# Second block's keys and queries read in fp32 by the SP queue and cast on chip, and the last piece stored from the scalar queue: sliding-window ALiBi attention followed by a squared-ReLU MLP

## The chip, the cores and the metric

The kernel runs on one core of one Trainium2 chip. The metric is the device time of one execution in microseconds (us), the median over several runs. One further execution is recorded by the hardware profiler; its page and its trace are what the text reads. PE is TensorE (matrix multiplies; PEld its weight loads), DVE is VectorE, ACT is ScalarE, POOL is GpSimd, SP is SyncE. A q behind a name is the queue of instructions that starts DMA transfers.

## The reference

Attention with 8 batches, 8 heads, 576 positions and a head size of 64, in a window of 128 positions with an ALiBi bias; its output, as 4608 tokens of 512 values, goes through an MLP with 2048 hidden values:

```python
scores = scale * np.matmul(q, k.transpose(0, 1, 3, 2))
rel = pos[:, None] - pos[None, :]
bias = slopes[:, None, None] * (-np.abs(rel).astype(np.float32))[None, :, :]
mask = (rel >= 0) & (rel < window)
scores = np.where(mask, scores + bias[None], -1000000000.0)
attn = softmax(scores)
x = np.matmul(attn, v)      # heads side by side: (4608, 512)
h = x @ w_in                # (4608, 2048)
r = np.maximum(h, 0.0)
out = ((r * r) @ w_out).astype(np.float32)
```

All inputs and the output are fp32 in memory.

## The kernel before, in words

**Blocks.** Each batch's 576 positions are cut into four blocks of 128 and one of 64. The list `seq` (L197 to L207) has the first blocks of all 8 batches first (numbers m = 0 to 7), then, for two batches at a time, their three middle blocks each ("full" jobs, which see the block before them too) and at last both 64-row ends together (one "half" job). `ranges` gives the order of the 36 tiles of 128 rows in which the MLP takes them; a tile of two halves is two places of 64 rows in the output.

**Attention of a block.** Its k and q go into a bf16 tile `kq`, its v into `vf` or `vt`. For m from 1 on, POOL issues these loads (L387, L392), and its DMA casts fp32 to bf16 on the way. Block 0 differs (`split`, L358 to L382): its k and q are read as fp32 into the tile `stage`, in two halves each, one issued by SP and one by ACT (L373), and DVE casts them into `kq` (L379). k and q are then transposed: for m below `N_PE` by PE with an identity (L443) and copies out of PSUM (L271 on DVE, L273 on ACT), for later blocks by a DMA transpose that SP issues (L429). The scores (L499) go through an exponential on ACT (L523) and a product with a mask on DVE (L531). P times v (L566) has a column of ones that gives the sum, by which DVE divides (L584, L588). The result `x` is transposed into `xT`, by PE (L608) and a copy for m below `N_PE`, in two cuts for m below `N_CUT`, and by a DMA transpose (L596) for the others.

**MLP.** It runs over 9 groups of 512 tokens. The up projection (`h`: L700 in group 0 by units of 128 tokens and 512 hidden values, in groups 1 and 2 by units of 256 tokens; L716 for the later groups) is followed by a ReLU on ACT (L671) and a square on DVE (L662) into `g`. The down projection (`o`, L742) of a tile has four parts of four matmuls, one for each quarter of w_out. A finished tile is copied to `osb` by DVE or ACT (L271, L273) and stored by SP (L761). The last tile is cut at column 384 (`CUT`) into two pieces, each with its own copy and stores. The weights come in four pieces each, cast by POOL's DMA (L340, L343).

**Order.** [...] A planner in the kernel file (class `Plan`) goes through all tasks with estimated durations and writes out one order for each engine. A task has the engines it may run on, a key (a due time, lower first), the tasks it needs and the buffers it takes and frees. On each engine the one with the lowest key is taken among those that could start within `NEAR` ns of the earliest; `LEAD` and `DUE` make the keys of attention blocks, `FIRST` (L16) is the order of the first loads on POOL. Up to eight casting DMAs are in flight in the plan (`LANES`). Where the plan has a hole on PE in its first 30 us, matmuls on a zero tile `warm` (L252) fill part of it. Each engine runs its instructions strictly in that order, with waits on semaphores.

Of the kernel before, what the change touches and what calls it, by code (L numbers as in the profile page):

```python
# [8 lines left out]
FP32 = mybir.dt.float32  # L9
# [5 lines left out]

FIRST = ["b0", "b1", "b2", "i0", "i1", "o0", "i2", "o1", "b3", "i3", "o2", "o3", "b4", "b5", "b6", "b7"]  # L16
DIAG = [[0], [1], [2], [3], [4, 5], [6, 7]]
N_PE = 9
N_CUT = 4
N_PVH = 1  # L20
N_WARM = 8
FILL = 0.7
LEAD = 320
IOTA = 3
# [3 lines left out]
SIZE = {"kq": 4, "v": 9, "kqT": 7, "P": 3, "x": 3}  # L28
DUE = {**{m: 200.0 * m - 1e5 for m in range(40)}, **{7: -40.0}}

# [26 lines left out]
class Plan:  # L57
# [7 lines left out]
    LANES = 8  # L65
    NEAR = {"PE": 25, "ACT": 250, "DVE": 60}
    FILL_UNTIL = 30000.0
# [15 lines left out]

    def order(self):
        used = {tag: [] for tag in self.bufs}
        free, cand, left = {}, {}, {}
# [89 lines left out]
def kernel(  # L176
    ctx: ExitStack, tc: tile.TileContext, q, k, v, moe_w_in, moe_w_out, out
):
    nc = tc.nc
# [20 lines left out]
    for b in range(0, B, 2):  # L200
        for x in [(b + i, kb) for i in range(2) for kb in range(1, HALF)]:
            jobs.append(("full", [len(seq)]))
            seq.append(x)
            ranges.append([x])
        jobs.append(("half", [len(seq), len(seq) + 1]))
        ranges.append([(b, HALF), (b + 1, HALF)])
        seq += ranges[-1]  # L207
    at = {x: m for m, x in enumerate(seq)}
# [27 lines left out]
    xt = ring("x", size["x"], [128, d_model])  # L236
    stage = const.tile([128, 2 * d_model], FP32)

# [18 lines left out]
    def act(n):  # L257
        return n * 0.95 + 115.0
# [43 lines left out]

    t_dist, t_mask, last_mask = [None, None], [[], []], None
    for part in (1, 0):
        key = EARLY + 2 if part else -1e5 + 1100
        t_dist[part] = plan.add({"DVE": 430.0}, key, lambda part=part: build_dist(part), [t_ident], name="dist",
                                later=0.0 if part else 18000.0)
        for p in range(H):
            def build_mask(p=p, part=part):
                nc.scalar.activation(masks[:, p, part], dist[:, part], AF.Exp, bias=0.0,  # L310
                                     scale=-(2.0 ** (-8.0 * (head_at[p] + 1) / H)))
            t_mask[part].append(plan.add({"ACT": act(128)}, key + 1 + p, build_mask, [t_dist[part]], name="mask"))

    def ones(ts):
        for t in ts:
            nc.vector.memset(t[:, :, D:D + 1], 1.0)
    t_ones = [plan.add({"DVE": 320.0}, EARLY + 3, lambda: ones(tiles["v0"][0:2]), name="ones"),
              plan.add({"DVE": 900.0}, -1e5 + 300, lambda: ones(tiles["v0"][2:]), name="ones", later=11000.0),
              plan.add({"DVE": 1200.0}, -1e5 + 900, lambda: ones(tiles["v"]), name="ones", later=20000.0)]

# [36 lines left out]
    def load_block(m, key):  # L357
        kb = seq[m][1]  # L358
        n = blk[kb]
        ns = 870.0 * n / 128  # L360
        split = m == 0
        s_kq[m], s_v[m] = Slot("kq"), Slot("v" if kb else "v0")
# [4 lines left out]

        if m == 0:
            t_l = []
            for i, src in enumerate((k, q)):  # L370
                for r, (eng, e) in enumerate((("SP", nc.sync), ("ACTQ", nc.scalar))):
                    def fetch(i=i, src=src, r=r, e=e):
                        e.dma_start(view(stage, i)[:, r], source(src, m, split)[:, :, r])  # L373
                    t_l.append(plan.add({eng: 450.0}, key + 0.1 * i, fetch, dma=330.0, lat=1000.0,
                                        name=f"l{'kq'[i]}{m}.{r}"))

            def cast_kq(i):
                w = slice(i * d_model, (i + 1) * d_model)
                nc.vector.tensor_copy(kq[s_kq[m].idx][:, w].rearrange("s (i r d) -> s r i d", i=4, d=D),  # L379
                                      stage[:, w].rearrange("s (r i d) -> s r i d", r=2, d=D))  # L380
            c_k = plan.add({"DVE": 480.0}, key, lambda: cast_kq(0), t_l[0:2], [s_kq[m]], name=f"ck{m}")
            c_q = plan.add({"DVE": 480.0}, key, lambda: cast_kq(1), t_l[2:4] + [c_k], name=f"cq{m}")  # L382
            t_kq[m] = [c_k, c_q]
# [38 lines left out]
    def transpose_kq(m, due):  # L422
        n = blk[seq[m][1]]
        kb = seq[m][1]
        sT = s_kqT[m] = Slot("kqT" if kb else "kqT0")
        split = m == 0
        if m >= N_PE:
# [7 lines left out]
        for i in range(2):  # L435
# [14 lines left out]
            for c0, c1 in pieces:  # L450
                def evac(i=i, st=st, c0=c0, c1=c1, e=len(evs[i])):
# [4 lines left out]
                    else:  # L456
# [3 lines left out]
                evs[i].append(plan.add({"ACT": act(w), "DVE": dve_p(w, 1 if split else 2)}, due - 58, evac,  # L460
                                       [t_tp[i]] + evs[i], [], [st], name=f"ev{m}.{i}"))
        last["tp"] = t_tp[1]
# [175 lines left out]
    def blocks(lo, hi):  # L638
        return [at[x] for r in range(lo // 128, hi // 128) for x in ranges[r]]
# [10 lines left out]

    g_slots, g_sq, o_slots = {}, {}, {}

    def relu_square(g, slot, last_mm, key, out_of, fused):
# [12 lines left out]
        else:  # L666
            srt = Slot("rt")

            def relu():
                srt.tile = work.tile([128, 512], BF16, tag="rt", bufs=3, name="rt")  # L670
                nc.scalar.activation(srt.tile, slot.tile, AF.Relu, bias=0.0, scale=1.0)  # L671
            tr = plan.add({"ACT": act(512)}, key, relu, [last_mm], [srt], [slot], name=f"relu{g}")
            ts = plan.add({"DVE": dve(512, 2)}, key, lambda: square(srt.tile), [tr] + g_sq[g][:1], [], [srt],
                          name=f"sq{g}")
        g_sq[g].append(ts)
# [10 lines left out]
    def unit(g, r, e, key):  # L686
# [8 lines left out]
        def emit():  # L695
            fill(t_mm, bank_of(slot, "h"))
            for f in range(nf):
                fc = nf * e + f
                for cc in range(C):
                    nc.tensor.matmul(slot.tile[:, f * w:(f + 1) * w], w_in_sb[:, cc, fc * 128:(fc + 1) * 128],  # L700
                                     xT[:, cc, lo:lo + w], start=cc == 0, stop=cc == C - 1)
        t_mm = plan.add({"PE": 4 * nf * mm(w)}, key, emit,
                        [t_win[nf * e // 4]] + [x for m in ms for x in t_x[m]], [slot] + new, name=f"u{g}.{r}.{e}")
        ts = relu_square(g, slot, t_mm, key,
# [4 lines left out]
    def fc_step(g, fc, key):  # L709
# [3 lines left out]
        def emit():  # L713
            bank(slot, "h")
            for cc in range(C):
                nc.tensor.matmul(slot.tile, w_in_sb[:, cc, fc * 128:(fc + 1) * 128],  # L716
                                 xT[:, cc, g * 512:(g + 1) * 512], start=cc == 0, stop=cc == C - 1)
        t = plan.add({"PE": 4 * mm(512)}, key, emit,
                     [t_win[fc // 4]] + [x for m in blocks(g * 512, g * 512 + 512) for x in t_x[m]], [slot] + new,
                     name=f"fc{g}.{fc}")  # L720
        ts = relu_square(g, slot, t, key, lambda gt: gt[:, fc, :], FUSED(g, fc))
# [10 lines left out]
    def o_piece(g, t, some, key, z, lo, hi, end):  # L732
# [4 lines left out]
        def emit():  # L737
# [3 lines left out]
            for fc in range(4 * some[0], 4 * some[-1] + 4):  # L741
# [3 lines left out]
                      [prev] + [x for p in some for x in [t_wout[p]] + sq_of[g, t, p]],  # L745
                      [slot] if some[0] == 0 else [], [g_slots[g]] if t == 3 and some[-1] == 3 and end else [],
                      name=f"o{g}.{t}.{some[-1]}")
        o_slots[g, t, z][1] = tm
# [4 lines left out]
        def evac():  # L753
            so.tile = work.tile([128, d_model], FP32, tag="osb", bufs=3, name="osb")
            copy(te, so.tile[:, 0:hi - lo], slot.tile[:, 0:hi - lo])
        te = plan.add({"ACT": act(hi - lo), "DVE": dve_p(hi - lo)}, key, evac, [tm], [so], [slot], name=f"oe{g}.{t}")

        def store():
            for i, (b, kb) in enumerate(ranges[4 * g + t]):
                n = blk[kb]  # L760
                nc.sync.dma_start(out[b * S + kb * 128:b * S + kb * 128 + n, lo:hi],  # L761
                                  so.tile[i * 64:i * 64 + n, 0:hi - lo])
        plan.add({"SP": 530.0}, key, store, [te], [], [so], dma=680.0 * (hi - lo) / 512, lat=1000.0, name=f"st{g}.{t}")

# [38 lines left out]
```

The softmax here doesn't subtract the row's maximum and nothing guards it: scores larger than these inputs give would overflow.

## Time and profile before

| | |
|---|---|
| median of 5 runs | 317.56 us (317.14 to 317.71) |
| the profiled execution's own time | 317.25 us |
| its span, first to last instruction | 315.5 us |
| PE, DVE, ACT, POOL busy | 306.4, 173.1, 173.5, 105.5 us |
| DMA packets | 164130, of which 154752 under 512 B |
| first matmul of the up projection | 14.07 us |
| last matmul | ends at 310.8 us |

The page has the busy time of each engine, the span in 40 slices, the DMA queues, the chain of work that ended last, and groups of instructions by line. Other views of the same trace are a timeline, the waits of an engine (who waited for whom, total us, times, longest us) and busy times in stretches of one's choice. A matmul's end is modelled by the profiler, so that PE can be busy without running at its peak; the step from one matmul's start to the next one's tells its true cost. In lists of DMA, MB count the bytes written.

### The profile page before, as it was taken

To read this page: it belongs to the slowest core of one execution; us is meant where nothing else is said; L and a number is where in the kernel's file an instruction comes from. 1 tells how busy PE (TensorE), PEld (TensorE's weight loads), DVE (VectorE), ACT (ScalarE), POOL (GpSimd) and SP (SyncE) were. 2 spreads that over 40 slices of the span, in tenths; PEclk is the share of its full clock that TensorE was granted. 3 is DMA by queue.
4 is the path that set the end of the run, shared out by engine and by line. 5 is a ranking of instruction groups with operands and counts; after the bars stand their busy time and mean duration, and the time that the engine had idled before them with its cause. 6 is when DMAs were issued, how large, how long until landed. Compare 5 with 4: busy or idle time off the path is not lost.

```text
span 315.5 us, 7140 instructions
## 1 busy us (share of the span) xinstructions
PE 306.4 (97%) x2810; PEld 176.4 (56%) x2810; DVE 173.1 (55%) x494; ACT 173.5 (55%) x340; POOL 105.5 (33%) x131
## 2 busy tenths in 40 slices
PE   6999999999999999999999999999999999999994
PEld 3877768667777655555554455545444444444442
DVE  3755577566767667676666666666663222222111
ACT  4675466668566636675656665547743444444300
POOL 8825498643623845206746007200000000000000
PEclk9999999999999999999999999999999999999998
DMA  9999999999999999959999949962211000011112
GB/s 130 189 202 190 170 195 175 145 168 144 221 160 129 179 165 177 156 96 140 167 195 164 138 98 132 193 115 70 50 52 50 35 34 33 35 33 45 56 69 67
DMA packets 164130, 39.14 MB, mean 124 GB/s; under 512 B 154752, under 2 KB 159616, under 8 KB 164096
## 3 DMA queue, kind: packets, MB, share of 16 engines
q0 software_dynamic: 114656, 18.10, 84.3%
q1 hardware_dynamic: 49152, 20.33, 33.4%
q8 instruction: 22, 0.36, 0.5%
q10 hardware_dynamic: 288, 0.26, 0.3%
q14 instruction: 12, 0.10, 0.1%
HBM read 36.70 MB, written 9.44 MB: 146 GB/s over the span
## 4 chain that ended last, share of the span: by engine, by line
PE 88%; DMA 8%; POOL 2%; issue 0%; DVE 0%; POOLq 0%
PE o L742 39%; PE h L716 27%; PE h L700 11%; PE pv L566 6%; PE s L499 5%; DMA w_out_sb<-in_moe_w_out_dram 5%; DMA w_in_sb<-in_moe_w_in_dram 3%; POOL kq L387 1%; POOL vf L392 1%; PE tp L443 1%; PE xp L608 0%; POOL w_in_sb L340 0%; POOL dist L287 0%; DVE osb L271 0%; POOLq L287 0%
## 5 line engine op out<-in xcount | busy, mean ns | idle before, releaser
L742 PE MATMUL o<-w_out_sb,g 128*128 128x512 bf16 (+2 forms) x592 | 143.0, 373 | 0.3 <-DMA w_out_sb<-in_moe_w_out_dram 0.3
L671 ACT ACTIVATE rt<-h 128x512 bf16<-128x512 f32 x144 | 85.8, 609 | 94.5 <-PE h L716 69.9
L662 DVE TENSOR_TENSOR g<-rt 128x512 bf16<-128x512 bf16 x144 | 60.2, 421 | 75.9 <-ACT rt L671 75.8
L716 PE MATMUL h<-xT,w_in_sb 128*128 128x512 bf16 x384 | 96.7, 379 | 0.0
L742 PEld LDWEIGHTS <-g 128*128 128x128 bf16 x592 | 54.1, 98 | 56.0 <-issue 0.4
L523 ACT ACTIVATE P<-s 128x512 bf16<-128x512 f32 (+1 forms) x136 | 67.0, 582 | 9.2 <-PE s L499 9.2
L716 PEld LDWEIGHTS <-w_in_sb 128*128 128x128 bf16 x384 | 35.2, 98 | 39.3
L531 DVE TENSOR_TENSOR P<-P,masks 128x512 bf16<-128x512 bf16 (+1 forms) x112 | 44.6, 405 | 15.7 <-ACT P L523 11.0
L700 PE MATMUL h<-xT,w_in_sb 128*128 128x128 bf16 (+1 forms) x512 | 46.7, 246 | 1.2 <-DMA w_in_sb<-in_moe_w_in_dram 0.7
L392 POOL DMA_DIRECT2D vt<-in_v_dram x32 | 27.1, 849 | 49.5 <-PE pv L566 46.5
L387 POOL DMA_DIRECT2D kq<-in_k_dram x39 | 33.4, 857 | 30.4 <-DMA kqT<-kq 23.8
L700 PEld LDWEIGHTS <-w_in_sb 128*128 128x128 bf16 x512 | 38.6, 98 | 5.2 <-DMA w_in_sb<-in_moe_w_in_dram 1.6
L387 POOL DMA_DIRECT2D kq<-in_q_dram x39 | 33.6, 861 | 8.8 <-DMA w_out_sb<-in_moe_w_out_dram 5.2
L588 DVE TENSOR_TENSOR x<-pv,rec 128x256 bf16<-128x256 f32 (+1 forms) x80 | 33.6, 422 | 2.6
L566 PEld LDWEIGHTS <-P 128*128 128x128 bf16 (+1 forms) x576 | 25.7, 101 | 15.3 <-DVE x L588 1.7
L584 DVE RECIPROCAL rec<-pv 128x4 f32<-128x4 f32 (+1 forms) x80 | 14.3, 179 | 20.9 <-PE pv L566 18.0
L566 PE MATMUL pv<-vt,P 128*128 128x65 bf16 (+1 forms) x448 | 24.6, 194 | 0.0
L273 ACT ACTIVATE osb<-o 128x512 f32<-128x512 f32 x23 | 13.9, 606 | 8.0 <-PE o L742 7.7
L499 PEld LDWEIGHTS <-kqT 64*128 64x128 bf16 x448 | 12.4, 94 | 7.3 <-issue 7.2
L271 DVE COPY osb<-o 128x512 f32<-128x512 f32 (+2 forms) x14 | 9.2, 654 | 12.8 <-PE o L742 12.6
L499 PE MATMUL s<-kqT 64*128 64x128 bf16 (+1 forms) x256 | 15.6, 210 | 0.0
L499 PE MATMUL s<-kqT,kqT 64*128 64x128 bf16 (+1 forms) x192 | 11.4, 209 | 0.0
(42 smaller groups left out, 102.6 us busy)
## 6 DMA issues: line engine op xcount, KB each, us to landing
out_dram<-osb SPq DMA_DIRECT2D x32, 256.0 KB, 4.0
kq<-in_k_dram POOLq DMA_DIRECT2D x31, 128.0 KB, 7.0
kq<-in_q_dram POOLq DMA_DIRECT2D x31, 128.0 KB, 7.2
vt<-in_v_dram POOLq DMA_DIRECT2D x24, 128.0 KB, 7.2
w_in_sb<-in_moe_w_in_dram POOLq DMA_DIRECT2D x4, 512.0 KB, 10.1
w_out_sb<-in_moe_w_out_dram POOLq DMA_DIRECT2D x4, 512.0 KB, 15.1
vf<-in_v_dram POOLq DMA_DIRECT2D x8, 128.0 KB, 6.2
out_dram<-osb SPq DMA_DIRECT2D x6, 128.0 KB, 2.3
```

The lines of the kernel that those rows point to most:

```text
L387: nc.gpsimd.dma_start(view(kq[s_kq[m].idx], i), source(src, m, split))
L392: nc.gpsimd.dma_start(tile_of(s_v[m])[0:n, :, 0:D], source(v, m))
L499: nc.tensor.matmul(sS[2 * g2 + r].tile[:, jj * 256 + c0:jj * 256 + c0 + w], tile_of(s_kqT[mk])[rows, c, :], tile_of(s_kqT[mq])[rows, C + c ...
L523: nc.scalar.activation(flat(Pt[sP.idx]), sS[i].tile.rearrange("p (j t) -> p j t", j=2)[:, :, lo:hi], AF.Exp, bias=0.0, scale=scale)
L531: nc.vector.tensor_tensor(flat(Pt[sP.idx]), flat(Pt[sP.idx]), flat(masks), op=ALU.mult)
L566: nc.tensor.matmul(sv.tile[0:n, hi * (D + 1):(hi + 1) * (D + 1)], Pt[sP.idx][:, place(h)].rearrange("p t q -> p (t q)")[:, w], tile_of(s_v ...
L588: nc.vector.tensor_tensor(xt[sx.idx][0:n, hf * 256:(hf + 1) * 256].rearrange("p (h e) -> p h e", h=4), heads(sv)[0:n, :, 0:D], sr.tile[0:n ...
L662: nc.vector.tensor_tensor(o, i, i, op=ALU.mult)
L671: nc.scalar.activation(srt.tile, slot.tile, AF.Relu, bias=0.0, scale=1.0)
L700: nc.tensor.matmul(slot.tile[:, f * w:(f + 1) * w], w_in_sb[:, cc, fc * 128:(fc + 1) * 128], xT[:, cc, lo:lo + w], start=cc == 0, stop=cc ...
L716: nc.tensor.matmul(slot.tile, w_in_sb[:, cc, fc * 128:(fc + 1) * 128], xT[:, cc, g * 512:(g + 1) * 512], start=cc == 0, stop=cc == C - 1)
L742: nc.tensor.matmul(slot.tile[:, 0:hi - lo], gt[:, fc, t * 128:(t + 1) * 128], w_out_sb[:, fc, lo:hi], start=fc == 0, stop=fc == FCB - 1)
```

## The change

- `split` holds for blocks 0 and 1 (`N_HW` = 2). Block 1's k and q are read as fp32 in two halves each, all four issued by SP, into a second `stage` tile. DVE or ACT casts them. POOL issues only the v of block 1.
- The first loads come in another order: the second piece of w_out and block 3 go ahead of the third piece of w_in.
- `N_PE` goes from 9 to 8, `N_CUT` from 4 to 2, `N_PVH` from 1 to 2 (P times v of block 1 takes a PSUM bank of tag h), `LEAD` from 320 to 440, and `NEAR` is 60 for PE and 0 for ACT. Block 7 loses its own due time.
- A table `ADJ` shifts the keys of some tasks by name. Tasks get distinct names for that.
- For the last two batches the tile of two halves goes one place ahead, so the last tile of all is a full block of 128 rows.
- The last piece of the last tile (columns 384 to 511) is copied by ACT alone and stored from ACT's queue.
- In the plan, a group's first up projection is ordered ahead of its other ones, and `g` is freed only when all four tiles of its group are done.

```diff
-FIRST = ["b0", "b1", "b2", "i0", "i1", "o0", "i2", "o1", "b3", "i3", "o2", "o3", "b4", "b5", "b6", "b7"]
+FIRST = ["b0", "b1", "b2", "i0", "i1", "o0", "o1", "b3", "i2", "i3", "o2", "o3", "b4", "b5", "b6", "b7"]
-N_PE = 9
-N_CUT = 4
-N_PVH = 1
+N_HW = 2
+N_PE = 8
+N_CUT = 2
+N_PVH = 2
-LEAD = 320
+LEAD = 440
-DUE = {**{m: 200.0 * m - 1e5 for m in range(40)}, **{7: -40.0}}
+DUE = {m: 200.0 * m - 1e5 for m in range(40)}
+ADJ = {
+    "ck1": 8900391.0, "e0.3": 100080.3, "e3.2": -142.3, "e3.3": -200, "e6.2": -40, "m1.0": 401.3, "m1.3": 99828.3,
+    "m2.2": 99627.1, "o1.2.0": -479.21, "o2.3.3": -535.5, "pv2.0": -398.2, "r7.0": 789.7, "squ0.0.2": -99571.3,
+    "squ0.1.2": -99827.9, "squ0.2.2": -99869.7, "xp5.0": 98961.41,
+}
-    NEAR = {"PE": 25, "ACT": 250, "DVE": 60}
+    NEAR = {"PE": 60, "ACT": 0, "DVE": 60}
     def order(self):
+        for t in self.tasks:
+            t.key += ADJ.get(t.name, 0.0)
...
-        ranges.append([(b, HALF), (b + 1, HALF)])
-        seq += ranges[-1]
+        seq += [(b, HALF), (b + 1, HALF)]
+        ranges.insert(len(ranges) - (b + 2 == B), seq[-2:])
...
-        split = m == 0
+        split = m < N_HW
...
-                for r, (eng, e) in enumerate((("SP", nc.sync), ("ACTQ", nc.scalar))):
+                for r, (eng, e) in enumerate((("SP", nc.sync), ("SP", nc.sync) if m else ("ACTQ", nc.scalar))):
...
-                nc.vector.tensor_copy(kq[s_kq[m].idx][:, w].rearrange("s (i r d) -> s r i d", i=4, d=D),
-                                      stage[:, w].rearrange("s (r i d) -> s r i d", r=2, d=D))
+                copy((c_k, c_q)[i],
+                     kq[s_kq[m].idx][:, w].rearrange("s (i r d) -> s r i d", i=4, d=D),
+                     stage[:, w].rearrange("s (r i d) -> s r i d", r=2, d=D))
+            engs = {"DVE": 480.0, "ACT": 600.0} if m else {"DVE": 480.0}
...
+        if end and (g, t) == (NG - 1, 3):
+            del engs["DVE"]
...
+        final = end and (g, t) == (NG - 1, 3)
...
-                nc.sync.dma_start(out[b * S + kb * 128:b * S + kb * 128 + n, lo:hi],
-                                  so.tile[i * 64:i * 64 + n, 0:hi - lo])
+                (nc.scalar if final else nc.sync).dma_start(
+                    out[b * S + kb * 128:b * S + kb * 128 + n, lo:hi], so.tile[i * 64:i * 64 + n, 0:hi - lo])
```

## The prediction, made before the changed kernel was run

> **What bounds the kernel now.** I read the page's engine rows first, then what the PE (TensorE) waited for, then the PE by stages of the early part, then the tail.
>
> ```profile
> span 315.5 us, 7140 instructions
> PE 306.4 (97%) x2810; PEld 176.4 (56%) x2810; DVE 173.1 (55%) x494; ACT 173.5 (55%) x340; POOL 105.5 (33%) x131
> ```
>
> PE is the bound; DVE and ACT have 45% spare. But a busy PE need not be doing useful work, so count the work: in the chain of waits four 512-column matmuls take 0.86 us (0.216 each) when nothing stands in their way, and sixteen 128-column ones 0.89 (0.056 each). At these prices PE is without work for 11.5 us up to 14.0, for 3.0 us from 14 to 36, and then for some 0.2 us in each 8 us, up to its last matmul at 310.8. So three stretches can give time back: before the first weights, the 3 us behind them, and the tail.
>
> The waits of PE in the second stretch, and PE in three of its 2 us stages (columns: stage, length, busy, clock, DMA share, GB/s):
>
> ```profile
> PE h L700 <- DMA w_in_sb<-in_moe_w_in_dram: 0.7, 1, 0.7
> PE h L700 <- ACT rt L671: 0.6, 1, 0.6
> PE o L742 <- DMA w_out_sb<-in_moe_w_out_dram: 0.3, 1, 0.3
> ...
> 20.00:22.00 2.00, 1.42 (x10) 1.00 1.24 205
> ...
> 28.00:30.00 2.00, 1.35 (x27) 1.00 1.24 206
> ...
> 32.00:34.00 2.00, 1.69 (x23) 1.00 1.40 205
> ```
>
> Each hole ends when a piece of weights has landed (w_in pieces land at 14.0, 16.6, 21.9, 30.0; w_out at 19.4, 25.1, 32.5, 35.9). The DMA engines never rest meanwhile: the early stage is set by delivery, in the order in which POOL issues. From 36 us PE alone is the bound.
>
> The tail, by the timeline:
>
> ```profile
> 310.56 1.13 SPq L761 DMA_DIRECT2D out_dram<-osb  x2
> 310.87 0.29 DVE L271 COPY osb<-o 128x128 f32<-128x128 f32 x1 [0.33 <-PE o L742]
> ...
> 311.79 1.19 SPq L761 DMA_DIRECT2D out_dram<-osb  x2
> ```
>
> The last copy ends at 311.16, but its two stores stand behind the two of the larger piece on SP; the last is issued at 312.39, lands at 314.30, and 1.16 us of closing steps make 315.46. Outside the span lie 1.75 us (317.25 profiled); the median is 0.31 above the profiled time, and I carry that along.
>
> **The tail edit.** The last tile becomes a full block, so each of its two pieces is one store of 128 rows in place of two of 64; and the last piece is copied and stored by ACT. The ACT copy of 128 columns is not in the trace: 0.383 us for 256 and 0.606 for 512 give 0.27 by a straight line, against 0.29 on DVE. ACT's queue then has nothing ahead of the store: issue at about 311.2. A 128-row store on SP lands 1.97 us after issue (issued 308.15, landed 310.13), so this one at 313.15 instead of 314.30: **-1.15 us**. The trace has no store from ACT; its nearest row is ACT's first load, landed 2.5 us after issue against 2.2 for the slowest store of this tail, which makes the smaller end -0.85. The larger is -1.4: four of the closing semaphore waits, 0.06 us each, come after the last landing now, and could be done before it. Nothing stands behind it on ACT.
>
> **Block 8 from PE to DMA transposes** (`N_PE` 9 to 8). Removes 8 transposes L443 and 4 of L608, 12 x 0.056 = **-0.67 us**, in a stage where PE is saturated, so all of it counts. It adds two DMA transposes on SP (1.2 to 2.7 us of SP each here), where SP has a store at 47.88 and the next transpose at 51.40. The price is delay: transposes issued at 51.4 to 64.1 land 8.6 to 9.3 us later. Block 8's q lands at 48.75; issued then, its kqT would be there at 57.4 to 58.0, while its scores now run at 55.51. Block 9, already on that route, lands at 60.03 for scores at 62.31, 2.3 us spare, so the written-out order does leave room for it. I take no stall; bounds 0 and +3.9 us (scores placed only the planner's own 5.05 us, 1150 + 1700 + 2200 ns in its constants, behind 48.75).
>
> **Block 1 by SP.** POOL loses two issues (0.89 + 0.90 us), so what stands behind moves up 1.8 us: v of block 1, k, q, v of block 2, and w_in piece 0 (issued 7.66, then about 5.9). SP gains four issues of 0.68 to 0.81 us, about 2.3 to 5.3, behind its two of block 0; its next work was at 39.17, so it is free. What counts is transfer time:
>
> ```profile
> DMA packets 341, 0.32 MB, mean 264 GB/s; under 512 B 32, under 2 KB 341, under 8 KB 341
> q10 hardware_dynamic: 197, 0.19, 56.7%
> ...
> DMA packets 5490, 0.69 MB, mean 154 GB/s; under 512 B 5490, under 2 KB 5490, under 8 KB 5490
> ```
>
> The first two lines are 2.2 to 3.4 us, block 0's fp32 reads; the last is 5.5 to 10, POOL's casting reads. MB are bytes written. Block 1's k and q cost 256 KB in 128 B packets at 154, 1.7 us (the landings step by 0.83 to 0.84 each). In fp32 they are 512 KB in 1 KB packets: 2.0 us at the mean of 264, 1.4 at the 375 of that window's full slices. Here a rule speaks against the edit. The Trainium skill, *DMA: Bandwidth & Descriptors*, "Issuing engines are not separate DMA queues", says that all issuers share the same 16 engines, and a second issuer saves issue time alone. By it nothing but 1.7 becoming 2.0 counts, +0.3 us, since the engines are full from 5 us on. The rows add that they are not full at 2 to 4 (the page's DMA share there is 7 tenths), where SP's new issues begin; and that the packets are eight times larger. I take 1.5 us for the two transfers, w_in piece 0 landing at 13.8 instead of 14.02: **-0.2** (bounds -0.6, +0.5).
>
> The two casts (0.67 and 0.43 us for block 0) go to DVE or ACT; DVE is idle from 6.93 to 8.73 and ACT from 5.1 to 7.04. Without that cover 1.1 us fall on block 1's chain. SP's second load went through, beside POOL's, at 81 packets in half a us (4.5 to 5.0), 0.8 us for its 128 packets; four more from 5.8 end at 9.0 to 9.6, with the cast at about 10.0, where block 1's q now starts its transposes at 9.5: 0.5 later. Block 2's loads, two POOL places earlier, land about 1 us sooner (9.6 to 11.3 now). I set these against each other.
>
> **The order of weights.** Pieces of weights step by 2.56 us, a block's k, q, v by 0.84 each. From 13.8 the new order gives: w_in 0 13.8, w_in 1 16.4, w_out 0 19.0, w_out 1 21.6, block 3 24.1, w_in 2 26.7, w_in 3 29.3, w_out 2 31.8, w_out 3 34.4. Work on hand: six units of blocks 0 to 2 (0.93 each, 5.6) and attention left over (1.2) fill 13.8 to about 20.6; two o parts with w_out 0 (1.73; the o tag has two banks) to 22.3; two with w_out 1 to 24.1; block 3's transposes and scores (0.9) to 25.0; then a hole until w_in 2 at 26.7, 1.7 us less block 3's pv and xp (0.5). From there three units, block 3's three, and w_in 3's four (9.3 us) bridge to w_out 3. That is about 1.2 of holes, and I add 1.2 for chain latencies like those at 14 to 16 and 20 to 22 now: 2.4 against 3.0, **-0.6 us** (bounds -1.6, +1.2; the nearest row is the old stretch, so I stay close to it). A second rule bears on that hole: *TensorE: Matmul & The Clock Gate*, "Part 1", lets the clock fall to half after an idle window of some 3.4 us. The rows know only holes of up to 0.7 us by PE's waits, and 0.056 us per matmul right after them. Taken at its word, the estimated hole of 1.7 stays under the window, and nothing is added; if it grew past it, 3.4 us at half clock would cost another 1.7.
>
> Edits that cost nothing: one cut less for x of blocks 2 and 3 (two copies of 0.38 become one of 0.60, off PE), pv of block 1 in the h banks (units don't need them before 14), the larger lead (attention is through at 232, 80 us ahead of the end), and the small keys, which reorder work on ACT and DVE within their 45% spare.
>
> **Sum.** -1.15 - 0.67 - 0.2 - 0.6 = -2.62: 317.25 to 314.63 profiled, 314.9 as a median.
>
> **Rivals.**
> (a) The reads are hidden anyway: delivery stays as it is, the start gives nothing, tail and transposes stay: 317.56 - 1.82 = 315.7. For it: the skill's rule, and full engines from 5 us. Against: the slack at 2 to 4 us.
> (b) The front closes further: both lower bounds, -0.6 and -1.6, give 317.56 - 1.82 - 2.2 = 313.5. For it: block 2 arrives sooner, and 3.0 us are there to take. Against: the first 11.5 us hardly move.
> (c) Block 1 arrives late. SP's second load landed 2.2 us behind its first (5.81 after 3.61). If four more step by 1.25 in place of 0.8 to 0.95, q lands at 10.8, is cast at 11.2, and PE, in order, stands at its transposes with block 0's rest behind them: 1.7 later than 9.5, so 317.56 - 1.82 + 1.7 = 317.4. Against: ACT's second load, on an equal queue, kept up with 1.1 us.
> (d) Slower: PE stands at block 8's scores for its DMA transpose. At the full 3.9 us: 314.9 + 3.9 = 318.8. It decides from 3.3 us on (2.62 and 0.64 for the 0.2%). For it: 8.6 to 9.3 us to landing and strict order on PE. Against: no wait of PE for any of the 31 transposes in the trace.
>
> **How the numbers follow.** Forecast 38% (314.1 to 315.5), (a) 22%, (b) 14%, (c) 14%, (d) 12%, each in all its sizes. 0.2%, 0.64 us, is what a measurement here can tell from no change. Faster: the first three (0.74) and some of (c) and (d), 0.80; same 0.08; slower 0.12. The range 313.4 to 317.8 leaves out the far half of (b), most of (d) and the far end of (c); the likeliest case's own is 314.1 to 315.5.
>
> **What would show it.** Tail: the 4.6 us from the last matmul's end (310.83) to the end of the span become 3.5, with one store from ACT's queue. Transposes: 64 matmuls that write tp, not 72, and no wait of PE for kqT. Start: w_in piece 0 landing at 13.8 and PE's last hole before 27. Wrong if PE's waits show DMA kqT, DVE or ACT on block 1, or a granted clock below 1.00 before 300 us.

## The result, and the profile after

The changed kernel takes 316.44 us (median of 23 runs, 315.93 to 318.41). The kernel before, in 41 runs beside it, takes 317.43 us (316.97 to 317.95). The ratio is 0.9975, with a 95% interval of 0.9968 to 0.9982: faster by a quarter of a percent, which the ratio puts at 0.8 us (the two medians are 0.99 apart). The forecast was a gain of 2.62 us and a time of 314.9 us, so the sign was right and the size was not.

The profiled execution of the changed kernel took 316.51 us, close to the median, so its trace can be read as a typical run. The first lines of its page:

```profile
span 314.7 us, 7132 instructions
PE 305.6 (97%) x2800; PEld 174.6 (55%) x2800; DVE 173.2 (55%) x496; ACT 171.6 (55%) x335; POOL 103.8 (33%) x129
```

PE is still the bound. Twelve transposes went from it (64 matmuls write tp, where there were 72), and the number of fillers on `warm` changed. What PE waited for, longest first (columns: total us, times, longest):

```profile
PE h L714 <- DMA xT<-x: 1.3, 1, 1.3
PE wm L427 <- DVE warm L301: 1.2, 1, 1.2
PE tp L457 <- ACT kq L283: 0.8, 1, 0.8
PE xp L622 <- ACT xT L283: 0.5, 1, 0.5
PE h L714 <- DMA w_in_sb<-in_moe_w_in_dram: 0.4, 2, 0.3
```

The waits for weights have shrunk, as the new order was to do. But the first line is new: the kernel before has no wait for a DMA transpose at all. The PE timeline of the changed kernel says where it is:

```profile
76.94 1.90 PE L759 MATMUL o<-w_out_sb,g 128*128 128x512 bf16 x8
80.12 1.03 PE L714 MATMUL h<-xT,w_in_sb 128*128 128x256 bf16 x8 [1.28 <-DMA xT<-x]
```

The PE stands before the first up projection of group 2, which reads blocks 8 and 9, until block 9's transposed `x` has landed. The queue of SP in that stretch, first in the changed kernel:

```profile
62.80 1.25 SPq L443 DMA_TRANSPOSE kqT<-kq  x1
64.14 1.27 SPq L610 DMA_TRANSPOSE xT<-x  x1
72.56 1.24 SPq L443 DMA_TRANSPOSE kqT<-kq  x1
73.89 1.50 SPq L610 DMA_TRANSPOSE xT<-x  x1
```

and in the kernel before:

```profile
64.10 1.34 SPq L429 DMA_TRANSPOSE kqT<-kq  x1
67.68 1.25 SPq L596 DMA_TRANSPOSE xT<-x  x1
```

The kqT at 72.56 (before: at 64.10) is block 12's, and the xT behind it is block 9's. Its x was ready at 69.03, but SP works in order and stood at block 12's kqT, whose q landed only at 72.51. So the xT was issued 6.2 us later than before and landed at 79.98 instead of 77.21. Why block 12's q was late is on POOL's queue. Its two loads in the kernel before, and then in the changed one:

```profile
51.88 0.90 POOL L387 DMA_DIRECT2D kq<-in_k_dram  x1
52.74 0.91 POOL L387 DMA_DIRECT2D kq<-in_q_dram  x1
```

```profile
61.19 0.88 POOL L401 DMA_DIRECT2D kq<-in_k_dram  x1 [1.34 <-DMA kq<-in_k_dram]
63.35 0.87 POOL L401 DMA_DIRECT2D kq<-in_q_dram  x1 [1.28 <-DMA kq<-in_q_dram]
```

There are four `kq` buffers, and block 12 takes the one of block 8. PE transposes used to free it at about 49; the DMA transpose frees it at its landing, 55.78. The plan puts block 12's loads behind that, some ten us later than before. (The buffer is free 5.4 us before the first of them starts; that rest is the order of loads on POOL and POOL's own wait, shown in the line.)

The PE in the stages shown of before (columns: stage, length, busy, clock, DMA share, GB/s):

```profile
20.00:22.00 2.00, 2.00 (x20) 1.00 1.95 172
...
28.00:30.00 2.00, 2.00 (x44) 1.00 1.24 206
32.00:34.00 2.00, 2.00 (x28) 1.00 1.50 198
```

The three holes of the old stretch are closed. The new ones lie at 15.6 to 17.4, where block 1's P times v, transposes and first units follow each other with gaps (1.4 us in all). The tail:

```profile
310.16 0.56 DVE L281 COPY osb<-o 128x384 f32<-128x384 f32 x1 [1.85 <-PE o L759]
311.05 0.28 ACT L283 ACTIVATE osb<-o 128x128 f32<-128x128 f32 x1 [13.26 <-PE o L759]
311.36 0.35 ACTq L783 DMA_DIRECT2D out_dram<-osb  x1
```

The last store is issued at 311.36 and lands at 312.96, which is 2.16 us after the start of the last matmul; before it was 3.68 us. That is 1.52 us, more than the 1.15 foreseen: 1.21 by the earlier issue, 0.31 by a shorter way from issue to landing. Closing steps grew from 1.16 to 1.78 us: eight semaphore waits of 0.06 us come after the last landing in place of five, and GpSimd's last steps come later still.

**The sum of the two profiled spans.** I price matmuls as the prediction did (the other shapes by their usual step in these traces) and count the time without useful ones. Transposes -0.67; time lost up to 36 us 14.32 against 14.91, -0.59; the stage from 76 to 92 us +1.63, most of it the wait; other stages -0.19. Together the last matmul starts at 310.80 instead of 310.62, 0.18 later. Landing -1.52 and closing +0.62 then give 315.46 + 0.18 - 1.52 + 0.62 = 314.74. So in this one pair of executions the tail's net 0.90 is what is left: the 1.26 of the start and of block 8 went into the wait.

### The profile page after: what moved, and what is told of

Same layout as the page of the kernel before. It is cut to its first block, busy times and chain, and to the rows that moved or that the text cites. A ratio compares the mean times of both kernels' runs of the same rounds, so it can differ in the third digit from the quotient of the medians.

```text
span 314.7 us, 7132 instructions
## 1 busy us (share of the span) xinstructions
PE 305.6 (97%) x2800; PEld 174.6 (55%) x2800; DVE 173.2 (55%) x496; ACT 171.6 (55%) x335; POOL 103.8 (33%) x129
## 4 chain that ended last, share of the span: by engine, by line
PE 88%; DMA 7%; POOL 3%; issue 0%; ACT 0%; POOLq 0%
PE o L759 38%; PE h L732 27%; PE h L714 11%; PE pv L580 6%; PE s L513 5%; DMA w_in_sb<-in_moe_w_in_dram 5%; DMA xT<-x 2%; POOL vf L406 1%; POOL kq L401 1%; PE tp L457 1%; POOL w_in_sb L350 1%; POOL w_out_sb L353 0%; PE xp L622 0%; POOL dist L297 0%; ACT osb L283 0%
## 5 line engine op out<-in xcount | busy, mean ns | idle before, releaser
L759 PEld LDWEIGHTS <-g 128*128 128x128 bf16 x592 | 53.3, 98 | 54.1
L545 DVE TENSOR_TENSOR P<-P,masks 128x512 bf16<-128x512 bf16 (+1 forms) x112 | 43.9, 404 | 9.5 <-ACT P L537 4.6
L401 POOL DMA_DIRECT2D kq<-in_k_dram x38 | 32.6, 858 | 27.5 <-DMA kqT<-kq 20.2
L401 POOL DMA_DIRECT2D kq<-in_q_dram x38 | 32.6, 858 | 5.9 <-DMA w_out_sb<-in_moe_w_out_dram 1.7
L283 ACT ACTIVATE osb<-o 128x512 f32<-128x512 f32 (+1 forms) x24 | 14.1, 590 | 21.8 <-PE o L759 21.8
L281 DVE COPY osb<-o 128x512 f32<-128x512 f32 (+1 forms) x13 | 8.9, 682 | 13.6 <-PE o L759 13.6
L513 PE MATMUL s<-kqT 64*128 64x128 bf16 (+1 forms) x256 | 15.6, 210 | 0.0
```

Of the source, the lines that this page charges most:

```text
L401: nc.gpsimd.dma_start(view(kq[s_kq[m].idx], i), source(src, m, split))
L513: nc.tensor.matmul(sS[2 * g2 + r].tile[:, jj * 256 + c0:jj * 256 + c0 + w], tile_of(s_kqT[mk])[rows, c, :], tile_of(s_kqT[mq])[rows, C + c ...
L545: nc.vector.tensor_tensor(flat(Pt[sP.idx]), flat(Pt[sP.idx]), flat(masks), op=ALU.mult)
L759: nc.tensor.matmul(slot.tile[:, 0:hi - lo], gt[:, fc, t * 128:(t + 1) * 128], w_out_sb[:, fc, lo:hi], start=fc == 0, stop=fc == FCB - 1)
```

## The experiments

My theory after the two traces: the tail edit is worth all that the kernel gained, block 8's move is worth its 0.67 us only if nothing stands ahead of block 9's x on SP, and the start gives little. The rivals: the move lacks a buffer; the start is what loses; the store's own queue is what gains. Every kernel was timed beside the kernel before on the same chip, and ratios are to that.

**The tail alone.** The kernel before, with the full block as last tile, one store for a piece, the last piece copied and stored by ACT, and `g` freed as in the changed kernel.

```diff
-        ranges.append([(b, HALF), (b + 1, HALF)])
-        seq += ranges[-1]
+        seq += [(b, HALF), (b + 1, HALF)]
+        ranges.insert(len(ranges) - (b + 2 == B), seq[-2:])
...
+        final = end and (g, t) == (NG - 1, 3)
...
-                nc.sync.dma_start(out[b * S + kb * 128:b * S + kb * 128 + n, lo:hi],
+                (nc.scalar if final else nc.sync).dma_start(out[b * S + kb * 128:b * S + kb * 128 + n, lo:hi],
```

> The kernel before with the tail edit alone (last tile a full block, last piece copied and stored by ACT). By the prediction -1.15 us, ratio 0.9964; by the profile after, where from the last matmul to the end it is 3.94 us against 4.84, -0.9 us, ratio 0.9972.

Measured: 315.93 us, ratio 0.9953 (0.9941 to 0.9965). Its last matmul starts at 310.62 as before, its last store lands 2.12 us later, and the tail ends it. The timeline:

```profile
310.57 0.33 SPq L763 DMA_DIRECT2D out_dram<-osb  x1
310.88 0.28 ACT L273 ACTIVATE osb<-o 128x128 f32<-128x128 f32 x1 [13.26 <-PE o L742]
311.18 0.35 ACTq L763 DMA_DIRECT2D out_dram<-osb  x1
```

The tail edit alone is faster than the whole change, by 0.7 us: all else together costs that much. In the two profiles 0.56 of it are closing steps, 1.22 us here and 1.78 in the changed kernel, and 0.18 its later last matmul.

**The tail from SP's queue.** The changed kernel with its last store on SP.

```diff
-                (nc.scalar if final else nc.sync).dma_start(
+                nc.sync.dma_start(
```

> The changed kernel with its last store issued by SP instead of ACT (the copy stays on ACT); nothing else moves. The prediction's step: with one store per piece SP is free by 311.1, so the store is issued at 311.4 either way, and the queue itself is worth 0 to 0.1 us. In the changed kernel the last store lands at 312.96, but eight closing semaphore waits of 0.06 us follow it, since ACT's semaphore is waited for first. If that order is set by the queue, the SP store ends 0.2 to 0.4 us sooner, ratio to before 0.996 to 0.997; if the closing steps are the same whatever the queue, 0.9975.

Measured: 316.94 us, 0.9981 (0.9966 to 0.9997), not to be told from the changed kernel's 0.9975. The store lands 2.14 us after the last matmul's start, against 2.16 from ACT, and 1.58 us after its issue, against 1.60. So the queue is worth nothing here. What gained is that a piece is one store: one store stands ahead of the last one, not two, and no second half follows it. PE's wait for xT was 0.6 us in this profile, not 1.3: its start was 1.07 us later (by the third copy to `osb`), so PE came later to the same wait.

**Block 8 back on PE.** The changed kernel with `N_PE` 9.

```diff
-N_PE = 8
+N_PE = 9
```

> The changed kernel with block 8 back on PE (N_PE 9): the whole step undone. Both theories: PE's wait for xT is gone, -1.3 or so, and twelve transposes are back on PE, +0.67: 315.8, ratio 0.995. If the wait cost nothing in the end because PE has slack later, 317.1, ratio 0.9995.

Measured: 316.30 us, 0.9954 (0.9943 to 0.9966). No wait for xT is left. Undoing the step gains 0.7 us (0.0021) where the prediction had it lose 0.67. Closing steps took 1.33 us, 0.45 less than in the changed kernel, so some 0.2 are left for PE, with 0.5 either way by the two intervals: the wait took about what the transposes gave. The ratio is also that of the tail alone, whose closing is alike: the start's edits, which this kernel still has, are worth about nothing together.

**Block 8 alone.** The kernel before with `N_PE` 8 and nothing else.

```diff
-N_PE = 9
+N_PE = 8
```

> The kernel before with N_PE 8 alone. If the wait belongs to the step (buffer and queue): -0.67 and some 1.0 to 1.5 of wait for xT, ratio 1.001 to 1.003. If the wait comes only with the changed kernel's larger lead and new keys: no wait, -0.67, ratio 0.998.

Measured: 318.42 us, 1.0034 (1.0020 to 1.0048). PE's longest wait, and SP's queue:

```profile
PE h L700 <- DMA xT<-x: 2.7, 1, 2.7
```

```profile
73.29 1.24 SPq L429 DMA_TRANSPOSE kqT<-kq  x1
74.62 0.71 SPq L761 DMA_DIRECT2D out_dram<-osb  x1
75.42 1.22 SPq L596 DMA_TRANSPOSE xT<-x  x1
```

The same wait in the same place, with a store as well between block 12's kqT and block 9's xT. So the wait belongs to this edit, not to the rest. Closing steps took 1.04 us, as without the edit (1.16), so the 1.1 us are the wait and its consequences, less the transposes. The profiled execution was the slowest of twelve (320.78 us), so its 2.7 us need not be the usual wait.

**A fifth kq buffer.** The changed kernel, so that block 12 needn't wait for block 8's buffer.

```diff
-SIZE = {"kq": 4, "v": 9, "kqT": 7, "P": 3, "x": 3}
+SIZE = {"kq": 5, "v": 9, "kqT": 7, "P": 3, "x": 3}
```

> The changed kernel with five buffers for kq instead of four. Theory (a late buffer behind the held-up queue): block 12's k and q no longer wait for the buffer that block 8's DMA transpose frees at 55.8; they are issued near 52 instead of 61.2 to 63.4, SP is not held up before x of block 9, PE's 1.3 us wait is gone: 315.1, ratio 0.993. Rival (slow transposes): the wait stays, 316.4. The plan places other things anew too, so 0.3 either way is left open.

Measured: 318.85 us, 1.0038 (1.0025 to 1.0050): slower. Block 12's q did land earlier (66.42) and its kqT was issued at 66.47. But the plan now put block 13's kqT ahead of block 9's xT, and that one's q landed at 73.04:

```profile
73.09 1.23 SPq L443 DMA_TRANSPOSE kqT<-kq  x1
74.42 1.33 SPq L610 DMA_TRANSPOSE xT<-x  x1
```

So a missing buffer isn't the cause by itself: another late transpose took its place in the queue. After the wait, 2.0 us of it, the granted clock of PE fell to 0.50 (columns: stage, length, busy of PE, PEld, DVE, ACT and POOL, clock, DMA share, GB/s):

```profile
80.00:84.00 4.00, 2.01 (x22) 1.36 (x19) 1.21 (x4) 0.60 (x1) 1.53 (x2) 0.98 1.52 175
84.00:87.00 3.00, 3.00 (x27) 1.93 (x26) 0.72 (x2) 1.52 (x3) 0.69 (x2) 0.50 1.65 149
```

The clock isn't what makes this kernel slow, though: its five executions with a mean clock of 1.000 took 317.98 to 319.28 us. What costs the rest of the 2.4 us is open.

**Block 9's x ahead in the queue.** The changed kernel with these two SP instructions exchanged.

```diff
     done = plan.order()
+    late = next(t for t in done if t.name == "kqT12")
+    done.remove(late)
+    done.insert(1 + next(i for i, t in enumerate(done) if t.name == "x9"), late)
```

> The changed kernel with one pair of instructions exchanged on SP: block 9's x transpose ahead of block 12's kq transpose; PE, ACT, DVE and POOL keep their order. Theory (a queue held up): in the changed kernel x of block 9 is ready near 69 us but is issued at 73.9, since SP stands at block 12's kq transpose, whose q lands at 72.5. Exchanged, x is issued near 69 to 70, lands by 77.5, PE's 1.3 us wait before the first up projection of group 2 is gone: 1.3 us less than the changed kernel, 315.1, ratio to before 0.993. Rival (transposes are slow in this stage, whoever stands ahead): at 8.3 us to landing x comes at 78 to 79 all the same, the wait stays over 0.5 us, 316.2 to 316.4, ratio 0.996 to 0.9975.

Measured: 316.09 us, 0.9953 (0.9940 to 0.9966). The xT is issued at 70.91 and lands at 77.62, and PE's wait is gone; by the ratios 0.7 us came back. The closing steps are still 1.78 us. In the profiled run (317.08 us, the slowest of six) a stretch of half clock fell into the start, which the changed kernel's profile does not have; the stage 18 to 22 us of this kernel (columns as in the last one):

```profile
18.00:22.00 4.00, 4.00 (x47) 4.00 (x48) 1.99 (x8) 1.41 (x5) 1.48 (x2) 0.57 1.58 189
```

Its two runs with a mean clock of 0.999 and 1.000 took 315.72 and 315.47 us, the four with 0.993 to 0.995 316.08 or more.

**Block 8 and the queue on a quiet start.** This was made last, because the runs above left open what the move is worth by itself. The kernel before with the tail edit, `N_PE` 8, and block 12's kqT and the store behind block 9's xT.

```diff
-N_PE = 9
+N_PE = 8
...
     done = plan.order()
+    for name in ("st1.0", "kqT12"):
+        late = next(t for t in done if t.name == name)
+        done.remove(late)
+        done.insert(1 + next(i for i, t in enumerate(done) if t.name == "x9"), late)
```

> The kernel before with the tail edit and block 8 on DMA transposes (N_PE 8), and on SP's queue x of block 9 ahead of block 12's kqT and of the store between them. Theory (block 8's step is worth its 12 transposes, -0.67 us, and loses only through what stands ahead of x of block 9 on SP): no wait of PE for xT above 0.3 us, last matmul 0.67 us earlier than 310.62, about 309.95, and 0.2% below the kernel before with the tail edit alone, which was at 0.9953, so 0.993, 315.3 us. Rival (any move of block 8 off PE costs, because its transposes land late for more than one consumer): a wait of PE for kqT or xT of 1 us or more comes back elsewhere, and the ratio is 0.9955 or above. If the wait for xT is gone but the last matmul is not earlier, the twelve transposes were not all on the path.

Measured: 315.34 us, 0.9930 (0.9911 to 0.9949), the lowest ratio here. SP's queue, PE's waits and the last copy:

```profile
64.22 6.83 SPq L596 DMA_TRANSPOSE xT<-x  x2
73.04 1.25 SPq L429 DMA_TRANSPOSE kqT<-kq  x1
74.38 0.63 SPq L763 DMA_DIRECT2D out_dram<-osb  x1
```

```profile
PE tp L443 <- DVE kq L379: 1.9, 1, 1.9
PE wm L413 <- DVE warm L291: 1.2, 1, 1.2
PE h L700 <- DMA w_in_sb<-in_moe_w_in_dram: 1.2, 2, 0.6
PE o L742 <- issue: 0.8, 5, 0.2
```

```profile
310.47 0.28 ACT L273 ACTIVATE osb<-o 128x128 f32<-128x128 f32 x1 [13.26 <-PE o L742]
```

Block 9's xT is the second of the two in the first line, issued at 69.87. There is no wait for xT or kqT. The last copy starts at 310.47, against 310.88 with the tail alone; the third copy to `osb` ran 0.23 later in this execution (47.49 against 47.26), so what follows the start gained 0.64. The two ratios differ by 0.0023, 0.73 us, though their intervals just overlap. Closing steps were 1.11 us. So the 0.67 us of twelve transposes are there by the trace, the ratios agree within their noise, and the place in SP's queue decides whether one gets them.

**The parts of the start, undone one by one in the changed kernel.** First the reads of block 1 (`N_HW` 1), then the old `FIRST`, then the old `FIRST` in the kernel with the exchange on SP.

```diff
-N_HW = 2
+N_HW = 1
```

> The changed kernel with block 1's k and q read by POOL again (N_HW 1), the order of the weights kept. The prediction gave the fp32 reads 0.2 us, so this is 316.6, ratio 0.998. If block 2's earlier arrival carries the start, it loses 0.6 or more: 317.0, ratio 0.9994. If the reads only delay block 1 (SP's loads landed at 7.0, 8.2, 9.3 and 10.3 instead of 7.1 and 7.9), it gains: 316.0, ratio 0.996.

Measured: 316.63 us, 0.9975 (0.9963 to 0.9988): the same as with the reads. But its closing steps took 1.11 us, 0.67 less than in the changed kernel. So the reads gain an estimated 0.7 us of work in this plan (1.78 less 1.11, at equal ratios; the two intervals leave 0.5 either way), and the closing takes it back. The section on the hardware says how.

```diff
-FIRST = ["b0", "b1", "b2", "i0", "i1", "o0", "o1", "b3", "i2", "i3", "o2", "o3", "b4", "b5", "b6", "b7"]
+FIRST = ["b0", "b1", "b2", "i0", "i1", "o0", "i2", "o1", "b3", "i3", "o2", "o3", "b4", "b5", "b6", "b7"]
```

> The changed kernel with the old order of the first loads (third piece of w_in ahead of the second of w_out and block 3). The prediction gave the new order 0.6 us: 317.0, ratio 0.9994. If the order is worth nothing because delivery is the same in sum, 316.4, ratio 0.9975.

Measured: 319.55 us, 1.0057 (1.0034 to 1.0081), from 317.63 us with a mean clock of 0.999 to over 320 us with 0.989 to 0.994. Its profile, the fastest of twelve executions, loses 14.53 us up to 36 us, 0.2 more than the changed kernel's, and waits 1.8 us for block 9's xT. If most of the cost is not in the start, but in the wait and in what follows it, the exchange on SP must take it away. With it added, group 2 waits for no xT:

```diff
-FIRST = ["b0", "b1", "b2", "i0", "i1", "o0", "o1", "b3", "i2", "i3", "o2", "o3", "b4", "b5", "b6", "b7"]
+FIRST = ["b0", "b1", "b2", "i0", "i1", "o0", "i2", "o1", "b3", "i3", "o2", "o3", "b4", "b5", "b6", "b7"]
...
+    done.insert(1 + next(i for i, t in enumerate(done) if t.name == "x9"), late)
```

> The kernel of the exchanged pair on SP with the old order of the first loads. With the pair as it was, the old order cost 2.6 us, with a wait for xT of 1.8 us at 78 us and mean clocks down to 0.987. If that loss is the wait and the half clock behind it, the exchange takes it away: 0.9953 to 0.996. If the old order itself is that much slower at the start, 1.003.

Measured: 316.06 us, 0.9947 (0.9928 to 0.9967), against 316.09 with the new `FIRST`: the cost is gone. So without the wait the order of the weights is worth nothing here.

**The same parts alone, on the kernel before with the tail edit.** First the new `FIRST`; then the reads and casts of block 1, as in the changed kernel, with its key for the first cast.

```diff
-FIRST = ["b0", "b1", "b2", "i0", "i1", "o0", "i2", "o1", "b3", "i3", "o2", "o3", "b4", "b5", "b6", "b7"]
+FIRST = ["b0", "b1", "b2", "i0", "i1", "o0", "o1", "b3", "i2", "i3", "o2", "o3", "b4", "b5", "b6", "b7"]
```

> The kernel before with the tail edit and the new order of the first loads alone. The tail edit alone measured 0.9953. The prediction gave the order 0.6 us: ratio 0.9934. If the start is set by the sum of what is delivered, and not by its order, 0.9953. If block 3 ahead of the third piece of w_in leaves PE without work, over 0.9965.

Measured: 318.31 us, 1.0018 (1.0007 to 1.0028), so it costs 2.4 us against the tail alone. The copies to `osb` show when: from the ninth on, where both have done the same work, this kernel is 2.77 us late (112.24 against 109.47) and stays so to its end, so the loss is made earlier. In the trace the units for the third piece of w_in, which filled PE from 22.37 on with the tail alone, can't run before that piece lands at 28.00, and from 20 to 31 us PE has five holes, 2.05 us in all, against two with the tail alone, 1.06 in all. The rest of the 2.77 is not accounted for.

```diff
-        split = m == 0
+        split = m < 2
...
-                for r, (eng, e) in enumerate((("SP", nc.sync), ("ACTQ", nc.scalar))):
+                for r, (eng, e) in enumerate((("SP", nc.sync), ("SP", nc.sync) if m else ("ACTQ", nc.scalar))):
```

> The kernel before with the tail edit and block 1's fp32 reads by SP with the casts alone. The prediction gave the reads 0.2 us: ratio 0.9947. If they are worth nothing, as undoing them in the changed kernel says, 0.9953. If block 1's later arrival (q at 10.3 instead of 7.9) costs what block 2's earlier one doesn't return, 0.996 to 0.998.

Measured: 318.02 us, 1.0007 (0.9995 to 1.0019), 2.1 us more than the tail alone. It is 2.44 us late at the third copy and stays so. The timeline of PE has the largest hole:

```profile
16.31 0.28 PE L611 MATMUL xp<-ident,x 128*128 128x128 bf16 x2
16.43 0.33 PE L252 MATMUL h<-warm 128*128 128x128 bf16 x3
18.05 1.07 PE L703 MATMUL h<-xT,w_in_sb 128*128 128x128 bf16 x16 [1.29 <-DMA w_in_sb<-in_moe_w_in_dram]
```

Block 1's q lands at 10.62 here, and 8.27 with POOL's casting read. Its x is transposed from 16.31 on, 15.14 with the tail alone, where a unit of block 1 on the first piece of w_in then ran at 16.38. Here there is none to run, and PE waits for the second piece. That is rival (c), block 1 late; and the w_in piece 0 came no sooner, at 14.34 against 14.19.

The old `FIRST` and POOL's reads are each worth over 2 us in the old plan and, once the wait for xT is gone, nothing in the new one. What else differs between the two plans is the keys, `LEAD`, `NEAR`, `N_CUT` and `N_PVH`. That it is these that fit the order of PE to the new landings is argued, not shown: they were not changed alone.

**Matmuls against the half clock.** The exchange on SP, and 18 filler matmuls on `warm` around block 1's transposes of x, where PE has its holes.

```diff
                 fill(t_xp[z], bank_of(so, "xp"))
+                for _ in range((8, 10)[z] if m == 1 else 0):
+                    nc.tensor.matmul(so.tile[:, 0:128], warm[:, 0:128], warm[:, 0:128], start=True, stop=True)
```

> The kernel of the exchanged pair on SP, with 18 more matmuls on the zero tile ahead of block 1's two x transposes, where PE stood idle for 0.5 and 0.6 us near 16 to 17 us. Theory (the clock falls behind the holes at the start): in the exchanged kernel's executions with a mean clock of 0.993 to 0.995, 3.4 us at half clock near 18 us cost 0.5 to 1.5; the filler keeps the clock, all executions come out like its best ones, 315.5 to 315.7, ratio 0.9940. Rival (the spread is the transfers', not the clock's): the filler changes nothing, 316.1, ratio 0.9953.

Measured: 315.94 us, 0.9941 (0.9924 to 0.9958), against 0.9953 without them. The intervals overlap, so this is inconclusive. The half clock of its profile lies at 9.6 to 13.0, before the weights.

## Why the prediction was right or wrong

**The tail, -1.15 (bounds -0.85 to -1.4).** Right in its mechanism, too small. Alone it is worth 1.5 us by the ratio (0.0047 of 317.4) and by the landing. The term that was mis-sized is the store: I took the 1.97 us from issue to landing of a store of 512 columns. Stores of 384 took 1.82 to 1.87, and the last one, of 128, took 1.56 to 1.60, from SP (1.58) as from ACT. The step also gave ACT's empty queue a part of the merit, and it has none. In the changed kernel the closing steps took 0.6 us of it back: I had taken them as 1.16 for good, with four waits that might be done sooner; three more came, and POOL's last steps 0.4 later. This term was left out of the sum.

**Block 8, -0.67, "I take no stall" (bounds 0 and +3.9).** This is the step that failed. The 0.67 us were there, and the place where I looked for a stall, block 8's own scores, has none; its kqT landed at 55.78, earlier than the 57.4 I had allowed. What I left out is the queue that the transposes are moved into, and the buffer that they hold. Block 8's DMA transpose frees its `kq` buffer at its landing, block 12's loads follow that, and SP, in order, holds block 9's x behind block 12's kqT. The price is a wait of 1.3 us in the changed kernel and 2.7 us in the one profile of the edit alone, there with a stretch of half clock behind it. The step alone came out at +1.1 us; in the changed kernel, closing set aside, at some +0.2 (0.5 either way) in place of -0.67. Rival (d) had the right kind of stall at the wrong transpose, and its price of 3.9 us was too high.

**Block 1 by SP, -0.2 (bounds -0.6, +0.5).** Nothing in the changed kernel's time: an estimated 0.7 us of work gained, and as much lost in the closing steps, which the prediction left out here too. The gain did not come from where I put it, the weights' landing. The rule that the prediction weighs against the edit was right there: w_in piece 0 landed at 14.14, not 13.8, and block 2's three loads at 9.48, 10.75 and 11.63, where before they landed at 9.63, 10.46 and 11.30, although POOL issued them 1.7 us earlier. SP's four issues took 0.60 us each and the data landed at 7.00 to 10.27, in steps of 1.0 to 1.2; the 9.0 to 9.6 foreseen was 0.7 us too early. (ACT's second load came 1.4 us after its first, not the 1.1 that I held against rival (c).) One sign of being wrong did show: PE waits 0.8 us, up to 8.98, for ACT's cast of block 1's k, and the cast of q ends at 11.03 where I had 10.0. That is close to (c), block 1 late, but it lies ahead of the first weights, and (c)'s price of 1.7 us shows in the old plan alone. By the time measured, rival (a), nothing from the start, is what came out.

**The order of weights, -0.6 (bounds -1.6, +1.2).** The 3.0 us that I put between 14 and 36 is 3.4 when counted again. In the profile the start gave 0.59, of the 0.8 foreseen for this step and the one before it together. By the medians it gave nothing: 0.9954 with the new start and without block 8's move, 0.9953 with the old start. One execution was too little to read a start from. The order of PE up to the third copy to `osb` is the same in the changed kernel and in its versions with another SP order, another last store, a fifth buffer or `N_PE` 9, and that copy began at 46.68, 48.52 (with a stretch of half clock ahead of it), 47.75, 46.76 and 47.84. In four profiles of kernels with the old start it began at 47.15 to 47.49. The profile shown is the earliest of the five. Its last hole in the start ends at 27.23, where I had put it before 27.

**The clock.** I took nothing for it, since by the rule that the prediction cites a hole of 1.7 us was too short. For the start as shown that was right, but as a threshold on one hole the rule is too mild here: half clock came after waits of 2.0, 2.2 and 2.7 us in three kernels.

**Edits that cost nothing.** ACT is busy for 171.6 us (173.5 before) and DVE for 173.2 (173.1), and PE waits at most 0.8 us at a time for either, but for the `warm` tile at the start. The small keys were not without effect, though, if they are what makes the new start as good as the old.

**The sum.** Tail -1.5, closing +0.6, block 8 +0.2 and start -0.1 (the kernel with `N_PE` 9 against the tail alone, less the 0.1 by which its closing is longer) give -0.8, the measured gain; since closing and block 8's term are what the ratios leave, this is a bookkeeping and no second proof. With the queue in order, the old start and the old closing it is -1.5 - 0.7 = -2.2, as measured with block 8 and the queue on the old start, against the foreseen -2.62.

## What to carry to other kernels

When work is moved onto an in-order DMA queue, ask what stands behind it there and which buffer it holds until its landing, not only whether its own consumer waits. Here the damage was two blocks away, and moving one instruction ahead in the queue turned a loss of 1.1 us into a gain of 0.7. At the end of a kernel, count the stores that stand ahead of the last one: halving them was worth 1.5 us, and the queue that issued them nothing.

## What the runs showed of the hardware

**Half clock in fixed stretches.** The granted clock fell to 0.5 for 3.41 us at a time: at 83.88 to 87.29 us after the 2.0 us wait with five buffers, at 83.12 to 86.54 after the 2.7 us wait with block 8 alone, at 16.04 to 19.46 after a wait of 2.2 us for weights in the changed kernel with `N_HW` 1, and at 18.58 to 21.99 with block 9's x ahead, where no wait of PE just before was longer than 0.5. In these stretches a matmul of 256 columns steps by 0.213 us in place of 0.109, and one of 128 by 0.107 in place of 0.056. A stretch at full load thus costs about 1.7 us. In each profile the recorded changes of the clock lie whole multiples of 3.41 us apart. That it depends on how holes fall into such periods would fit, but was not tested. The changed kernel's own wait of 1.3 us brought none in its profile. Stretches at 8 to 13 us, before the weights, cost little: the kernel with the lowest ratio has one at 8.68.

**A piece of weights lands with its slowest part.** A transfer of 512 KB is signalled in 16 parts. In the fifteen profiles the second w_in piece landed at 16.59 (before) to 18.35 us, while its 15th part was there at 16.34 to 17.06. In each of them one 16 KB packet of the queue for instructions, of 0.95 to 0.98 us, starts at 14.4 to 15.9. In the kernel before, packets that start from 15 to 17 us (queue: packets, MB, their time as a share of 16 engines):

```profile
q0 software_dynamic: 402, 0.40, 120.6%
q8 instruction: 1, 0.02, 3.0%
```

The last part comes 0.2 to 1.6 us behind the 15th. That the instruction packet makes one engine late, and by chance one that was last already, fits these numbers but was not tested. It would account for the scatter of the start.

**Closing steps.** From the last landing to the end of the span it took 1.04 to 1.79 us, and this goes by the program: the changed kernel and five versions of it with `N_PE` 8 and block 1's reads took 1.77 to 1.79, and the one with five buffers 1.66. Those with `N_PE` 9 or without these reads, and the ones built on the kernel before, took 1.04 to 1.33. Two terms make it up. SP passes 2 to 8 semaphore waits of 0.06 us after the last landing. What follows them took 0.83 to 0.84 us in the six kernels without block 1's reads, and 1.15 to 1.28 in the nine with them. In these nine POOL has 200 to 202 instructions in the trace, and a hole of 0.34 to 0.37 us stands ahead of its 197th, whichever instruction that is, within the closing steps. In the six, POOL has 203 or 204, and its 197th comes no later than the first of the closing steps, without such a hole behind it. So the reads, which take two loads from POOL, move the hole into the end; why POOL stops there isn't shown. This makes 0.4 us of difference, and the waits 0.2, that no view of the work shows.
